# The last two heads' gradient stores cut into 120 and 8 partitions, in a decode transformer layer's forward and backward pass

## The chip, the cores and the metric

The kernel runs on one core of a Trainium2 chip. The metric is the time of one execution on the device in microseconds (us), as the median of the runs of a kernel. The engines are named as in the profile: PE (TensorE matmul), PEld (its weight load), DVE (VectorE), ACT (ScalarE), POOL (GpSimd) and SP (SyncE). SP, ACT and POOL also issue DMA transfers, each into a queue of its own, and 16 DMA engines carry out what the queues hold.

## The reference

One decoding step of a transformer layer for a batch of 4, with everything in bf16, forward and backward. Cut to what matters:

```
B=4, H=32 heads, Sk=4096 cached positions, Dh=128, D=512, F=1792
h   = x + softmax(q . k_cache / sqrt(Dh)) . v_cache @ wo,    q = layernorm(x) @ wq
out = h + (silu(n @ w1) * (n @ w3)) @ w2,                    n = layernorm(h)
returns out, and the gradients of x, k_cache, v_cache, wq, wo, w1, w3, w2 for grad_out
```

By bytes the caches are nearly all of it. k_cache and v_cache hold 4 x 32 heads of 4096 x 128 numbers, 1 MB per head and cache, so 128 MB each; k_cache is read once and v_cache twice, and the two gradients of the same size are written. The gradient of v_cache for a head is the outer product of the head's probabilities with the gradient of its attention output; that of k_cache is the outer product of the gradient of its scores with its query.

## The kernel before

A head's 4096 x 128 block is one SBUF tile of 128 partitions: partition p holds the positions 32p to 32p+31, which are 8 KB in a row in memory. Such a tile lies in a "slot" of SBUF; there are 22 slots, and a program-side list `free` says which ones can be given out again. The order of the instructions on each engine is the order in which the program writes them down.

The kernel has three stages. The first goes over all heads for the forward attention. The middle one computes the output projection and the feed-forward block, forward and backward. The third, which the change touches, goes once more over all 128 heads `s`, with batch index `b = s % 4` and head index `h = s // 4`; so the last two are b = 2 and 3 of h = 31. For every head:

- `prefetch` and `load_V2` (L749) load V for heads to come, from SP's queue.
- `front(s + 1)` transposes V of the next head on PE (L739), copies it back to SBUF on ACT (`V_T`, L740), and multiplies it on PE with the output gradient (L1070).
- `store_late(nc.scalar)` issues, from ACT's queue, the two stores of the head before: the gradient of v (`gv`, to `out_3`) and of k (`gk`, to `out_2`), 1 MB each (L1106). It then gives both slots free.
- `back(s)` forms `gv` and `gk` of this head on DVE (two outer products at L1077, and small steps at L1090 and L1093 between them) and appends them to `late`.
- Heads 0 and 1 are stored at once, from POOL's queue, in place of that.
- `step` puts in pieces of the weight gradients (`side_work`), whose stores of some 0.9 to 1 MB go from POOL's queue, besides two stores of 4 rows from SP's queue (L964 and L987).

After the last `back`, one more `store_late(nc.scalar)` issues the stores of head 127, and there is no work left for `step`.

A DMA instruction tells of its landing by a semaphore. Eight semaphores go round for the transfers of SP's and ACT's queues; before an issue the program waits until the transfer that had the same semaphore before, eight issues earlier, has landed. The last loads of V come well ahead of the end, so that at the end all eight go round among ACT's stores.

Of the kernel before, what the change touches and what calls it, by code (L numbers as in the profile page):

```python
# [24 lines left out]
def kernel(  # L25
# [23 lines left out]
    P = nc.NUM_PARTITIONS  # L49

    B = A_x.shape[0]
    D = A_x.shape[-1]
    H = A_k_cache.shape[1]
# [33 lines left out]
    def rows_of(ap):  # L87
        return ap.rearrange("(p j) d -> p j d", p=P)
# [83 lines left out]
    def ones_window(col):  # L172
# [11 lines left out]
                          in_=rowg[:, None, :, None].to_broadcast([P, 4, 8, 4]))  # L184
# [691 lines left out]
    with ExitStack() as c2:  # L876
# [226 lines left out]
        def store_late(eng):  # L1103
            b, h, gv, gk = late.popleft()
            for out_ap, sl in ((out_3, gv), (out_2, gk)):
                eng.dma_start(out=rows_of(out_ap[b, h]), in_=sl.heads())  # L1106
                sl.give()

        def prefetch(s):
# [6 lines left out]
        for s in range(NH):  # L1116
            prefetch(s + 1)
            if s + 1 < NH:
                if s + 1 not in V2s and s + 1 not in VTs:
                    load_V2()  # L1120
                front(s + 1)
            if late:
                store_late(nc.scalar)
            back(s)
            if s < 2:
                store_late(nc.gpsimd)
            if s >= S0:
                step("s", 1 if s < S0 + 44 else 2 + (s % 3 == 0))
        store_late(nc.scalar)
        step("s", 400)  # L1130

# [29 lines left out]
```

## Time and profile before

| | |
|---|---|
| runs (3) | 1748.7, 1748.4, 1747.94 us; median 1748.4 |
| profiled execution | 1748.7 us; span from its first to its last instruction 1746.9 us |
| busy share of the span | PE 76%, PEld 64%, DVE 72%, ACT 55%, POOL 16% |
| DMA | 707.85 MB, mean 405 GB/s |
| share of the 16 DMA engines' span by queue | q1 (SP's) 59.5%, q10 (ACT's) 36.4%, q0 (POOL's) 2.5%, instruction pages 0.6% |
| mean TensorE clock granted | 0.75 |

How to read it. The shares are means over three stages with different limits; what the change is worth is read from the end of the third stage. The page cuts the span into 40 slices of 43.7 us and gives for each the busy tenths of the engines and of the DMA engines, and the bytes moved. The view of the DMA queues does the same for any stretch, cut into 40 slices, and names the transfers issued in it with their time from issue to landing. The timeline gives each instruction's start and duration; "ACTq" is ACT's sequencer, which waits and issues while the engine itself computes nothing.

### The profile page before, as it was taken

To read this page: it belongs to the slowest core of one execution; us is meant where nothing else is said; L and a number is where in the kernel's file an instruction comes from. 1 tells how busy PE (TensorE), PEld (TensorE's weight loads), DVE (VectorE), ACT (ScalarE), POOL (GpSimd) and SP (SyncE) were. 2 spreads that over 40 slices of the span, in tenths; PEclk is the share of its full clock that TensorE was granted. 3 is DMA by queue.
4 is the path that set the end of the run, shared out by engine and by line. 5 is a ranking of instruction groups with operands and counts; after the bars stand their busy time and mean duration, and the time that the engine had idled before them with its cause. 6 is when DMAs were issued, how large, how long until landed. Compare 5 with 4: busy or idle time off the path is not lost.

```text
span 1746.9 us, 43817 instructions
## 1 busy us (share of the span) xinstructions
PE 1324.8 (76%) x18993; PEld 1113.0 (64%) x18993; DVE 1253.1 (72%) x1382; ACT 956.8 (55%) x1463; POOL 278.9 (16%) x552
## 2 busy tenths in 40 slices
PE   5889888888888889877777876666868767766773
PEld 4667666677666667767776875554656555655563
DVE  5989899889998996555667577557466655656484
ACT  3455445445444544655555555556756666666663
POOL 2333333333333330100000000000000010011000
PEclk8999999999999999755555556676556655556555
DMA  9999999999999999789999999999999999999998
GB/s 398 410 418 418 419 418 419 419 412 418 417 416 397 418 407 360 287 356 411 418 413 404 422 418 412 388 397 395 425 424 419 401 414 413 411 423 417 417 415 343
DMA packets 107122, 707.85 MB, mean 405 GB/s; under 512 B 11232, under 2 KB 18920, under 8 KB 23984
## 3 DMA queue, kind: packets, MB, share of 16 engines
q1 hardware_dynamic: 67280, 422.68, 59.5%
q10 hardware_dynamic: 36288, 264.26, 36.4%
q0 software_dynamic: 3360, 18.11, 2.5%
q8 instruction: 149, 2.44, 0.5%
q14 instruction: 45, 0.37, 0.1%
HBM read 422.58 MB, written 282.34 MB: 404 GB/s over the span
## 4 chain that ended last, share of the span: by engine, by line
DMA 36%; ACT 10%; PE 9%; DVE 4%; issue 2%; ACTq 1%; SPq 0%; POOL 0%; DVEq 0%; POOLq 0%
DMA out_dram<-gk 15%; DMA out_dram<-gv 9%; ACT VT L740 7%; DMA V<-in_A_v_cache_dram 6%; PE pt_tps L739 4%; DMA wq<-in_A_wq_dram 2%; DVE gv L1077 2%; PE dq_ps L902 1%; DMA out_dram<-gwo 1%; PE rep_ps L1054 1%; DVE gk L1077 1%; ACTq L1106 1%; DMA w<-in_B_w_dram 1%; DMA w2a<-in_B_w_dram 1%; DMA out_dram<-gwq 1%
## 5 line engine op out<-in xcount | busy, mean ns | idle before, releaser
L740 ACT COPY VT<-pt_tps 128x1024 bf16<-128x1024 bf16 x512 | 491.9, 1016 | 212.9 <-PE pt_tps L739 132.9
L739 PE MATMUL pt_tps<-ident_b,V 128*128 128x128 bf16 x4096 | 451.1, 292 | 88.5 <-ACT VT L740 88.5
L739 PEld LDWEIGHTS <-V 128*128 128x128 bf16 x4096 | 401.0, 138 | 176.2 <-issue 160.5
L1077 DVE TENSOR_TENSOR gv<-P,reps 128x4096 bf16<-128x4096 bf16 x128 | 292.9, 2288 | 200.7 <-DMA out_dram<-gk 95.8
L1077 DVE TENSOR_TENSOR gk<-dS,reps 128x4096 bf16<-128x4096 bf16 x128 | 293.4, 2292 | 67.8 <-DMA out_dram<-gv 39.8
L421 DVE TENSOR_TENSOR PK<-Kn,PK 128x4096 bf16<-128x4096 bf16 x128 | 302.9, 2366 | 35.9 <-POOL PK L417 35.9
L436 PE MATMUL M_ps<-PK,Vn 128*128 128x130 bf16 x4096 | 285.4, 222 | 45.1 <-DMA Vn<-in_A_v_cache_dram 44.2
L436 PEld LDWEIGHTS <-Vn 128*128 128x128 bf16 x4096 | 252.4, 99 | 65.4 <-DMA Vn<-in_A_v_cache_dram 59.1
L328 DVE STREAM_TRANSPOSE KT<-Kn 128x512 f32<-128x512 f32 (+1 forms) x321 | 250.9, 798 | 0.5 <-issue 0.5
L323 ACT COPY KT<-pt_tps 128x1024 bf16<-128x1024 bf16 x128 | 129.4, 1012 | 186.9 <-PE pt_tps L322 155.3
L1070 PE MATMUL dP_ps<-dOT_bf,VT 128*128 128x1 bf16 x4096 | 152.4, 166 | 67.4 <-ACT VT L740 65.7
L1070 PEld LDWEIGHTS <-VT 128*128 128x128 bf16 x4096 | 141.0, 104 | 79.8 <-ACT VT L740 77.8
L336 POOL COPY zq<-qT_bf 128x2 bf16<-128x2 bf16 x128 | 152.3, 1190 | 0.0
L1073 POOL COPY P<-P_all 128x64 bf16<-128x64 bf16 x128 | 43.2, 352 | 592.9 <-DVE gv L1077 592.9
L417 POOL COPY PK<-P_all 128x64 bf16<-128x64 bf16 x128 | 32.4, 253 | 437.0 <-ACT P_all L411 431.7
L1090 DVE TENSOR_SCALAR dSt<-dP_ps,c_rep 128x32 f32<-128x32 f32 x128 | 31.6, 246 | 97.0 <-PE dP_ps L1070 96.8
L411 ACT COPY P_all<-pt_P 32x64 bf16<-32x64 bf16 x256 | 52.1, 203 | 58.0 <-PE pt_P L407 55.7
L322 PE MATMUL pt_tps<-ident_b,Kn 128*128 128x128 bf16 x1024 | 80.7, 223 | 0.7 <-DVE qrep L282 0.7
L446 PE MATMUL kP_ps<-PK,onesw 128*32 128x512 bf16 x1024 | 79.2, 386 | 0.0
L322 PEld LDWEIGHTS <-Kn 128*128 128x128 bf16 x1024 | 62.2, 100 | 26.5 <-issue 26.5
L1057 ACT CAST reps<-rep_ps 128x512 bf16<-128x512 f32 x64 | 37.5, 586 | 70.9 <-PE rep_ps L1054 59.7
L400 ACT ACTIVATE Pn<-E,rl 128x1024 bf16<-128x1024 f32 x64 | 73.7, 1152 | 2.8 <-DVE rl L397 2.8
(234 smaller groups left out, 1231.5 us busy)
## 6 DMA issues: line engine op xcount, KB each, us to landing
Kn<-in_A_k_cache_dram SPq DMA_DIRECT2D x128, 1024.0 KB, 14.9
Vn<-in_A_v_cache_dram SPq DMA_DIRECT2D x128, 1024.0 KB, 15.2
V<-in_A_v_cache_dram SPq DMA_DIRECT2D x128, 1024.0 KB, 10.6
out_dram<-gv ACTq DMA_DIRECT2D x126, 1024.0 KB, 12.8
out_dram<-gk ACTq DMA_DIRECT2D x126, 1024.0 KB, 15.3
wq<-in_A_wq_dram SPq DMA_DIRECT2D x8, 1024.0 KB, 11.1
out_dram<-gw POOLq DMA_DIRECT2D x6, 896.0 KB, 11.9
wo<-in_A_wo_dram SPq DMA_DIRECT2D x4, 1024.0 KB, 12.1
```

Of the source, the lines that this page charges most:

```text
L322: nc.tensor.transpose(pt[:, i, :], Kn[:, c * GW + i, :], ident_b[:])
L323: nc.scalar.copy(out=KT[:, c * GW:(c + 1) * GW, :], in_=pt[:])
L328: nc.vector.transpose(out=KT[:, c * w_:(c + n) * w_], in_=Kn[:, c * w_:(c + n) * w_])
L336: nc.gpsimd.tensor_copy(out=zq[gi % 2][hl][:, 32:132:67], in_=qT_bf[:, s:s + 1].to_broadcast([P, 2]))
L400: nc.scalar.activation(out=st["Pn"][:], in_=st["E"][:, :, None, :].to_broadcast([P, JQ, 4, 32]), func=AF.Copy, scale=rl[:])
L421: nc.vector.tensor_tensor(out=PK[:, :, 0:Dh].rearrange("p j (r t) -> p j r t", t=2), in0=Ks[s].heads().rearrange("p j (r t) -> p j r t", t=2),
L436: nc.tensor.matmul(hold["M"][:], lhsT=Vn[:, j, :], rhs=PK[:, j, :], start=(j == 0), stop=(j == SJ - 1))
L446: nc.tensor.matmul(hold["kP"][32 * q:32 * (q + 1), :, :], lhsT=ones_window(w), rhs=PK[:, j0:j0 + 4, 0:Dh], start=(w == 0 and c == 0), stop ...
L739: nc.tensor.transpose(pt[:, i, :], Vn[:, g * GW + i, :], ident_b[:])
L740: nc.scalar.copy(out=VT[:, g * GW:(g + 1) * GW, :], in_=pt[:])
L1070: nc.tensor.matmul(dP_ps[:, j:j + 1], lhsT=VT[:, j, :], rhs=dOT_bf[:, s:s + 1], start=True, stop=True)
L1077: nc.vector.tensor_tensor(out=dst.rearrange("p j (r t) -> p j r t", t=2), in0=col2[:, :, None, :].to_broadcast([P, SJ, Dh // 2, 2]), in1=r ...
```

## The change

The stores of the last two heads are each issued in two parts: partitions 0 to 119 and partitions 120 to 127. All other stores stay as they were. Where four DMA instructions were issued from ACT's queue at the end (gv and gk of heads 126 and 127), there are eight, each part of 120 rows followed by its part of 8 rows; the bytes, their places and the slots are the same. The lines behind the changed ones move down by 4, so that the store's line is L1106 before and L1110 after.

```diff
         def store_late(eng):
             b, h, gv, gk = late.popleft()
             for out_ap, sl in ((out_3, gv), (out_2, gk)):
-                eng.dma_start(out=rows_of(out_ap[b, h]), in_=sl.heads())
+                cut = [0, 120, P] if h == H - 1 and b >= B - 2 else [0, P]
+                for p0, p1 in zip(cut[:-1], cut[1:]):
+                    eng.dma_start(out=rows_of(out_ap[b, h])[p0:p1], in_=sl.heads()[p0:p1])
                 sl.give()
```

## The prediction

> **What bounds the kernel now.** I read the page's slices first, then its queue table, and then the last 47 us, because the change touches nothing earlier. In the page's second part one digit is a fortieth of the span (43.7 us).
>
> ```profile
> DMA  9999999999999999789999999999999999999998
> GB/s 398 410 418 418 419 418 419 419 412 418 417 416 397 418 407 360 287 356 411 418 413 404 422 418 412 388 397 395 425 424 419 401 414 413 411 423 417 417 415 343
> ...
> q10 hardware_dynamic: 36288, 264.26, 36.4%
> ```
>
> The DMA engines are at 9 tenths or more nearly throughout, so the kernel is bound by bytes, and nothing on PE, DVE, ACT or POOL counts at its end. Only the last slice is low: 343 GB/s against 415 to 417 before it. q10 is ACT's queue. It carries 252 stores of 128 rows: 252 x (128 packets of 8 KB + 16 closing packets) = 36288. So each of 16 engines gets 8 packets and one closing packet of every store.
>
> The timeline of ACT, 1711 to 1728 us, shows the last issues (start, time, what), the last six being gv and gk of heads 125, 126 and 127.
>
> ```profile
> 1721.13 0.34 ACTq L1106 DMA_DIRECT2D out_dram<-gv  x1
> 1721.16 1.04 ACT L740 COPY VT<-pt_tps 128x1024 bf16<-128x1024 bf16 x1
> 1721.56 0.93 ACTq L1106 DMA_DIRECT2D out_dram<-gk  x1
> 1722.59 1.33 ACTq L1106 DMA_DIRECT2D out_dram<-gv  x1
> 1724.01 1.17 ACTq L1106 DMA_DIRECT2D out_dram<-gk  x1
> 1725.27 1.19 ACTq L1106 DMA_DIRECT2D out_dram<-gv  x1
> 1726.56 1.21 ACTq L1106 DMA_DIRECT2D out_dram<-gk  x1
> ```
>
> DVE's last product starts at 1723.47 and takes 2.29 us. All that follows is storing. The DMA view of 1735 to 1747 us (slices of 0.3 us) shows how the storing ends, and that of 1740.95 to 1745.3 its last piece:
>
> ```profile
> GB/s 437 382 410 437 382 437 437 437 219 218 164 164 137 137 137 137 82 55 55 27 27 27 27 27 27 27 27 27 27 27 0 27 27 27 0 0 0 0 0 0
> DMA packets 226, 1.57 MB, mean 131 GB/s; under 512 B 34, under 2 KB 34, under 8 KB 34
> ```
>
> ```profile
> DMA packets 15, 0.11 MB, mean 24 GB/s; under 512 B 2, under 2 KB 2, under 8 KB 2
> ```
>
> One engine moves 27 GB/s (437/16). So eight engines are done by 1737.4, six are left at 1738.0, three at 1739.8, two at 1740.1, and from 1740.9 to 1745.2 one works alone. Its last 15 packets are 13 of 8 KB and two closing ones in 4.3 us, 0.31 us per 8 KB packet, which is the pace of the others: it isn't slow there, it is late, by about 13 packets against the second latest and 25 against the first eight. The last store was issued at 1726.56, and the DMA view of 1726 to 1728 gives its landing:
>
> ```profile
> out_dram<-gk ACTq DMA_DIRECT2D x1, 1024.0 KB, 19.1
> ```
>
> It lands at 1745.65, and the span ends 1.25 us later, at 1746.9. (Profiled execution: 1748.7; span plus 1.8. The runs' median is 1748.4, 0.3 lower. I subtract from the median.)
>
> **The change, part by part.** Four stores of 128 rows (gv and gk of heads 126 and 127) become four of 120 rows and four of 8. The program order says that nothing else moves: PE, DVE, POOL and SP have the same instructions, ACT has four issues more, at its very end.
>
> *Four issues more on ACT.* 4 x 0.34 to 1.33 us (rows above) = 1.4 to 5.3 us. ACT has nothing after its VT copy at 1721.16, and no engine waits for ACT any more. They cost nothing as long as packets are queued: the last store sits 19.1 us between issue and landing, where the first store of the phase, on idle engines (issued at 747.6), took 3.9 us.
>
> *The waits in front of them.* Eight completion semaphores go round, and an issue waits until the store eight issues earlier has landed. With eight issues where four were, this wait moves later: the 120 rows of head 127's gv wait for head 124's gv (issued 1716.58, 12.0 us to land: 1728.6), its 8 rows for head 124's gk (1717.02 + 14.0 = 1731.0), the 120 rows of gk for head 125's gv (between its neighbours, one store of 2.45 us apart: 1733.4), and its 8 rows for head 125's gk (1721.56 + 14.3 = 1735.9). Behind each on ACT stand only the remaining parts. An early engine asks for gk of head 127 about 8 x 0.306 = 2.45 us before its end at 1737.4, so at 1735.0. Issued at 1733.4, the packets are there about 0.9 us later (3.9 less 8 packets and a landing of 0.5) or, if the issue takes its 1.2 us, at 1735.5. Early engines may idle 0.5 us; they have 3.5 us to spare before 1740.9. The last 8 rows, issued at 1735.9, land by 1735.9 + 3.9 = 1739.8 even if they took as long as a whole store. So: 0 us, hidden by the late engines.
>
> *What the cut does to the engines.* This is the whole effect. A store of 128 rows runs on 16 engines. The page's packet count also tells of small ones: q1's 67280 packets come out only if the two stores of 4 rows (L964, L987) have 4 closing packets each, not 16. So the row count sets the number of engines, and the nearest rule through 128 on 16 and 4 on 4 is the largest number up to 16 that divides the rows: 120 on 15, 8 on 8. One engine then has no packet of the last four stores: 4 x (8 x 0.306 + 0.006) = 9.8 us less for it. Eight engines get one packet and a closing one more per store: 4 x 0.31 = 1.25 us more.
>
> If the engine left out is the late one, it ends at 1745.2 - 9.8 = 1735.4. The end is then set by the second latest: 1740.9 if it isn't among the eight, 1740.9 + 1.25 = 1742.2 if it is; between the two the third and fourth, from 1740.1 to 1740.4, plus 1.25, give up to 1741.6. Gain 3.05 to 4.3 us, middle 3.6. Following packets (each starts where the last one of its engine ended), I find that the engines of the 4-row store at L987 aren't those that also fetch instruction pages, and that the late one takes no such pages either and is none of those four, while the latest of the others does fetch them; if the eight include the four engines of that small store, the second latest is more likely not hit. I take 3.6: 1748.4 - 3.6 = 1744.8.
>
> The Trainium skill, DMA: Bandwidth & Descriptors, section "Rules for kernel authors", speaks against the change: two transfers to disjoint sets of partitions gain nothing, since both go over all 16 engines. By that rule the late engine keeps its load, and the sum is zero or a loss. The same page, section "Why a DMA increments its semaphore by 16 and not by 1", states the divisor rule (100 partitions on 10 engines) and that the lowest-numbered engines are taken; by it the engine left out is the last, number 15. Its section "Latency and other measured facts" says that engines 7 and 15 are usually the slower ones; the trace gives no numbers of engines, so it shows one late engine without saying which. With 15 the sum is the gain above; with 7 it is a loss of 1.25 us.
>
> What a measurement can tell from no change here is about 0.2%, 3.5 us; the runs of before lie within 0.8 us.
>
> **The rivals.**
>
> *A, forecast (0.70): the late engine is the one relieved.* For it: it keeps its lag through a stretch in which every engine works at the same pace, so its lag comes from its own history, and it is none of the small store's engines. Against: 14 others could be left out. 1744.1 to 1745.4, by itself with the runs' spread 1743.9 to 1745.6.
>
> *B (0.21): another engine is relieved.* The late one then keeps its 8 packets per store, and takes 4 x 0.31 us more if it is among the eight. 1748.4 to 1749.65. For it: the count of engines says nothing of which; a cut between rows 119 and 120 spares one engine only.
>
> *C, slower (0.09): 120 rows go to fewer than 15 engines.* If the number must be a power of two, 8 engines take 15 rows each. Their extra is 4 x (7 x 0.306 + 0.31) = 9.8 us: on the second latest 1740.9 + 9.8 = 1750.7, a span 5.5 us longer, 1753.9; on the late one itself 1758.2. It decides from 10 engines on: 12 rows each give 4 x (4 x 0.306 + 0.31) = 6.1 us, so the second latest ends at 1747.0, past 1745.2. Both known row counts, 128 and 4, are powers of two with powers of two for engines, so the page doesn't exclude it.
>
> **How the numbers follow.** The likeliest is A with 1744.8. In A the gain passes 3.5 us where the second latest isn't among the eight; I give that 0.49 of the 0.70. Faster 0.49, within 0.2% 0.21 + 0.21 = 0.42, slower 0.09. The range has to reach into B, since A alone is 0.70: from 1743.9 to 1749.6.
>
> **What would show it.** q10's packets count the engines: 36288 - 4 x 144 + 4 x (120 + 15) + 4 x (8 + 8) = 36316 for 15 and 8; 36352 if all parts go to 16; 36288 again for 8 and 8. In the DMA view of the end, the stretch of 27 GB/s alone should shrink from 4.3 us to about 1, and the last packet lie 3 to 4.3 us nearer to DVE's last product. I am wrong in the mechanism if that stretch stays at 4 us or more (B), and in the sum if ACT's last issue comes later than 1738 or the slices before 1737 fall below 400 GB/s: then the moved waits starve the engines.

## Result and profile after

The changed kernel is slower: 1754.62 us, the median of four runs (1753.77 to 1756.67), against 1748.55 us (1747.94 to 1749.19) before. The ratio is 1.0036, with a 95% interval of 1.0019 to 1.0054, so the loss is 6.1 us where a gain of 3.6 was forecast. The profiled execution took 1754.06 us, its span 1752.3.

These are the page's slices and ACT's queue of the changed kernel, to be laid beside the same lines of before.

```profile
DMA  9999999999999999689999999999999999999997
GB/s 398 409 419 418 419 418 419 419 415 418 413 417 394 418 407 356 275 358 416 417 419 413 422 418 409 392 382 417 425 423 411 401 411 405 420 419 416 418 415 298
...
q10 hardware_dynamic: 36316, 264.26, 36.5%
```

The queue has 36316 packets, the number that the prediction worked out for parts of 120 rows on 15 engines and parts of 8 rows on 8. So the engines were counted rightly. The last slice is at 298 GB/s in place of 343, and the slice before it is unchanged at 415: the loss is at the very end. (Slices 16 and 17, in the middle stage, differ too; the change issues nothing there.)

The timeline of ACT shows the last issues of the changed kernel (start, duration, instruction; x2 is a part of 120 rows and its part of 8).

```profile
1725.18 2.48 ACTq L1110 DMA_DIRECT2D out_dram<-gv  x2
1727.76 3.60 ACTq L1110 DMA_DIRECT2D out_dram<-gk  x2
1731.45 5.46 ACTq L1110 DMA_DIRECT2D out_dram<-gv  x2
1737.01 3.56 ACTq L1110 DMA_DIRECT2D out_dram<-gk  x2
```

Before, the last issue began at 1726.56. Now the last two lie between 1737.01 and 1740.57. The waits have moved as the prediction said, but they are longer than it worked out (it had the last at 1735.9). On DVE the last product starts later as well, in this execution. The first line is the kernel before, the second the changed one:

```profile
1723.47 2.29 DVE L1077 TENSOR_TENSOR gk<-dS,reps 128x4096 bf16<-128x4096 bf16 x1
1725.53 2.29 DVE L1077 TENSOR_TENSOR gk<-dS,reps 128x4096 bf16<-128x4096 bf16 x1
```

Of these 2.06 us, 1.6 are there already at the product before (1722.36 in place of 1720.73), and the rest is a wait for PE; the first part of the change is issued at 1725.18. In the profiles of the experiments the same product starts anywhere from 1722.48 to 1728.45. So profiles are compared below by their drain: the span's end less the start of this product. It is 23.43 us before and 26.77 us after, 3.3 us more.

The DMA views of the drain show where that comes from. The first fence is the kernel before from 1727 to 1737 us, the second the changed one from 1730 to 1742 us, in both while ACT's last stores are moving on nearly all engines.

```profile
DMA packets 584, 4.26 MB, mean 426 GB/s; under 512 B 64, under 2 KB 64, under 8 KB 64
## 3 DMA queue, kind: packets, MB, share of 16 engines
q10 hardware_dynamic: 584, 4.26, 101.5%
```

```profile
DMA packets 496, 3.51 MB, mean 293 GB/s; under 512 B 67, under 2 KB 67, under 8 KB 67
## 3 DMA queue, kind: packets, MB, share of 16 engines
q10 hardware_dynamic: 496, 3.51, 89.5%
```

Read the rate and the share at the end of the last line together. The engines are busy for 89.5% of this time, so they don't mainly wait for packets; yet they move 293 GB/s, not 426. What remains is that a packet takes longer. The share gives it: before, 1.015 x 16 engines x 10 us over 584 - 64 = 520 packets of 8 KB is 0.31 us each; after, 0.895 x 16 x 12 us over 429 is 0.40 us. That is a mean over the whole stretch, in which some stores of 128 rows are still on their way. It hides two kinds of packets: in the trace's list of packets, 292 of the 429 took less than 0.34 us, as all 520 did before, and the other 137 took longer, most often about 0.6 us.

The end of the drain, the changed kernel from 1741 to 1752 us in slices of 0.275 us:

```profile
GB/s 328 179 298 268 209 417 298 387 238 209 238 0 89 30 60 30 30 60 60 60 60 60 60 30 60 60 0 30 30 30 30 30 30 30 30 0 0 0 0 0
```

30 is one packet in a slice. Most engines are done at about 1744.5 and not at 1737.4; two engines go on to about 1748.1, and one alone to 1750.6.

### The profile page after: what moved, and what is told of

It is laid out like the page before. It is cut to its first block, busy times and chain, and to the rows that moved or that the text cites. A ratio compares the mean times of both kernels' runs of the same rounds, so it can differ in the third digit from the quotient of the medians.

```text
span 1752.3 us, 43821 instructions
## 1 busy us (share of the span) xinstructions
PE 1321.2 (75%) x18993; PEld 1116.8 (64%) x18993; DVE 1252.8 (71%) x1382; ACT 956.6 (55%) x1463; POOL 283.2 (16%) x552
## 3 DMA queue, kind: packets, MB, share of 16 engines
q10 hardware_dynamic: 36316, 264.26, 36.5%
q8 instruction: 149, 2.44, 0.5%
## 4 chain that ended last, share of the span: by engine, by line
DMA 36%; PE 10%; ACT 9%; DVE 5%; issue 2%; ACTq 1%; POOL 0%; DVEq 0%; SPq 0%
DMA out_dram<-gk 15%; DMA out_dram<-gv 11%; DMA V<-in_A_v_cache_dram 7%; ACT VT L740 7%; PE pt_tps L739 4%; DVE gv L1077 3%; DMA wq<-in_A_wq_dram 1%; DVE gk L1077 1%; DMA out_dram<-gwo 1%; PE dq_ps L902 1%; PE rep_ps L1054 1%; DMA w2a<-in_B_w_dram 1%; PE dP_ps L1070 1%; ACTq L1110 1%; PE M_ps L436 1%
## 5 line engine op out<-in xcount | busy, mean ns | idle before, releaser
L1073 POOL COPY P<-P_all 128x64 bf16<-128x64 bf16 x128 | 47.6, 386 | 592.7 <-DVE gv L1077 592.7
L354 PE MATMUL S_ps<-KT,W 128*32 128x256 bf16 x1536 | 74.6, 285 | 0.1
```

What stands on the lines that cost most here:

```text
L354: nc.tensor.matmul(st["S"][32 * c:32 * (c + 1), :], lhsT=lhsT, rhs=rhs, start=(hl == 0 and k == 0), stop=(hl == G - 1 and k == 3), tile_po ...
```

## Experiments

Each edit is one to the changed kernel, and concerns only the stores of the last two heads unless said. Three theories stood at first: the parts take longer because of how their rows lie over the engines ("spread"; with the later runs "ports", "dealing"); the moved waits starve the engines ("waits"); or nothing is slow, and the late engine is one of the eight that take a ninth packet ("late alone"). Each ratio is against the kernel before, run again beside the experiment: its median was 1748.81 us for the first four experiments, 1748.76 for the next four and 1748.3 for the last two.

**Parts of columns: eight issues and their waits, with 128 rows in each.**

```diff
-                cut = [0, 120, P] if h == H - 1 and b >= B - 2 else [0, P]
-                for p0, p1 in zip(cut[:-1], cut[1:]):
-                    eng.dma_start(out=rows_of(out_ap[b, h])[p0:p1], in_=sl.heads()[p0:p1])
+                cut = [0, 30, SJ] if h == H - 1 and b >= B - 2 else [0, SJ]
+                for j0, j1 in zip(cut[:-1], cut[1:]):
+                    eng.dma_start(out=rows_of(out_ap[b, h])[:, j0:j1], in_=sl.heads()[:, j0:j1])
```

> The stores of the last two heads are cut by columns instead of by partitions: 128 rows of 7.5 KB and 128 rows of 0.5 KB. There are again eight issues at the end, with the same semaphores and the same bytes in each part, but every part has 128 rows, so nothing changes in which engine takes which rows. Theory Spread (a store of 120 rows is slow because its rows fall on the engines otherwise than those of 128 rows do): 1748.5 to 1749.5 us, packets at their usual pace up to the end. Theory Waits (the waits that move later starve the engines): as the changed kernel, 1753.5 to 1755.5 us, with gaps between packets. Theory Late alone (the late engine is one of the eight that take the 8 rows, and nothing else): 1748.5 to 1749.5 us.

Measured: 1748.07 us, ratio 0.9997 (0.9988 to 1.0006), drain 21.16 us. It has the same eight issues, the same bytes in each part and the same waits behind eight semaphores, and no loss can be measured. Its last issues in the timeline, and its DMA view from 1728 to 1738 us:

```profile
1730.06 2.54 ACTq L1110 DMA_DIRECT2D out_dram<-gv  x2
1732.90 2.75 ACTq L1110 DMA_DIRECT2D out_dram<-gk  x2
```

```profile
DMA packets 951, 4.13 MB, mean 413 GB/s; under 512 B 107, under 2 KB 443, under 8 KB 836
```

413 GB/s. Its last pair begins at 1732.90 and not at 1737.01, since the stores that it waits for land sooner. So the late issues of the changed kernel are a consequence of slow packets and not their cause. The theory of the waits falls.

**The parts of 120 rows alone: rows 120 to 127 aren't stored.**

```diff
-                cut = [0, 120, P] if h == H - 1 and b >= B - 2 else [0, P]
+                cut = [0, 120] if h == H - 1 and b >= B - 2 else [0, P]
```

> The last two heads' stores have rows 0 to 119 only; rows 120 to 127 of those four blocks are left out. Four issues at the end, as before the change, so no wait moves, and no engine takes a ninth packet. Theory Spread: still slower than before, 1751 to 1753.5 us (1754.6 less 1.25 us for the ninth packets, and up to 2 us if the eight waits cost something too), with 8 KB packets of 0.6 us among those of 0.31. Theory Waits: 1748.5 us. Theory Late alone: 1748.5 us, because the late engine then has its 8 packets per store as before.

Measured: 1753.94 us, 1.0029 (1.0017 to 1.0041), drain 29.32 us. This kernel has as many issues as the kernel before, no wait moved, and 0.26 MB less to store; it loses nearly the whole, 0.4 us more than the range expected for "spread". So the waits and the ninth packets aren't needed for a loss. Its DMA view from 1727 to 1737 us:

```profile
DMA packets 447, 3.26 MB, mean 326 GB/s; under 512 B 49, under 2 KB 49, under 8 KB 49
```

**Cut at row 112: the parts of 112 and of 16 rows both run on 16 engines.**

```diff
-                cut = [0, 120, P] if h == H - 1 and b >= B - 2 else [0, P]
+                cut = [0, 112, P] if h == H - 1 and b >= B - 2 else [0, P]
```

> The cut lies at 112: 112 rows are 7 on each of 16 engines, 16 rows one on each, so every engine has 8 packets per head's block as before, but in eight issues, and with consecutive rows on an engine if that is how rows are dealt out whenever there aren't 128. Theory Spread by consecutive rows: slower than before, 1751 to 1755 us. If the 15 engines in place of 16 are what costs: 1748.5 to 1749.5 us. Theory Waits: 1753.5 to 1755.5 us. Theory Late alone: 1748.5 us, since no engine gets more than before.

Measured: 1754.66 us, 1.0034 (1.0023 to 1.0046), drain 26.82 us, and 36352 packets on the queue: 16 engines for both parts, and seven packets plus one, so eight for every engine, as before the change. Its DMA view from 1728 to 1740 us:

```profile
DMA packets 470, 3.11 MB, mean 259 GB/s; under 512 B 91, under 2 KB 91, under 8 KB 91
```

The loss is about that of the change. So a loss of this size needs neither an engine that is left out nor eight with one packet more: all engines have equal loads here, and are slow.

**Cut at row 64.**

```diff
-                cut = [0, 120, P] if h == H - 1 and b >= B - 2 else [0, P]
+                cut = [0, 64, P] if h == H - 1 and b >= B - 2 else [0, P]
```

> The cut lies at 64: each half is 4 rows on each of 16 engines, and each engine has 8 packets per block. The Trainium skill (SBUF: State Buffer, Door 1: the DMA port swizzle) states that partitions 0 to 63 lie behind 8 of the 16 ports and 64 to 127 behind the other 8, so that half the bandwidth is reached. Theory Spread through ports: a half's 4 rows take about 0.6 us per packet, so up to twice the 2.45 us per block while both halves keep in step: 1752 to 1758 us, more than with 120 and 8. Theory Spread by the engines' number alone: 1748.5 to 1749.5 us. Theory Waits: 1753.5 to 1755.5 us. Theory Late alone: 1748.5 us.

Measured: 1751.55 us, 1.0014 (1.0004 to 1.0024), drain 24.85 us. Slow again (270 GB/s from 1727 to 1739 us), but it costs less than the change, where more was expected: a miss in size. The two halves of a head were in flight together, and by the next two runs the lower half is slow by itself. That each half is slow for what it shares with itself and not with the other, and that this is why it costs less, is argued, not shown.

**The same size of store on two sets of partitions.** The first stores only rows 0 to 63 of the last two heads, the second only rows 32 to 95; the other rows aren't stored. Rows, bytes, issues and packets are the same (36032 on the queue in both).

```diff
-                cut = [0, 120, P] if h == H - 1 and b >= B - 2 else [0, P]
+                cut = [0, 64] if h == H - 1 and b >= B - 2 else [0, P]
```

> The last two heads' stores have partitions 0 to 63 only; 64 to 127 of those four blocks are left out. Four issues, 64 rows, 16 engines with 4 packets each. To be read beside the kernel with partitions 32 to 95. The Trainium skill (SBUF: State Buffer, Door 1: the DMA port swizzle) states that these rows lie behind 8 ports. Theory Ports: two engines meet at each port, 8 KB packets of 0.45 to 0.6 us in place of 0.31 while the four stores run, 200 to 300 GB/s. Theory Dealing (any row count other than 128 is dealt out in a way that costs, whichever rows): the same here as with partitions 32 to 95. Time with half of the last 4 MB left out: at the usual pace 1743.5 to 1744.5 us (the late engine has 16 packets fewer, 4.9 us); with slow packets 1744.5 to 1747.5.

```diff
-                cut = [0, 120, P] if h == H - 1 and b >= B - 2 else [0, P]
+                cut = [32, 96] if h == H - 1 and b >= B - 2 else [0, P]
```

> The last two heads' stores have partitions 32 to 95 only; the others of those four blocks are left out. Four issues, 64 rows, 16 engines with 4 packets each, as many bytes as with partitions 0 to 63. If rows are dealt out in order, four to an engine, engines 0 to 7 have partitions 32 to 63 and engines 8 to 15 partitions 64 to 95, which by the Trainium skill's table of ports (SBUF: State Buffer, Door 1: the DMA port swizzle) are 16 different ports, one for each engine. Theory Ports: packets at 0.31 us as with 128 rows, above 400 GB/s, and 1743.5 to 1744.5 us. Theory Dealing: packets as slow as with partitions 0 to 63, and the same time as that kernel.

Measured: 1746.93 us, 0.9986 (0.9976 to 0.9997), drain 22.98 us, for rows 0 to 63; 1745.46 us, 0.9977 (0.9966 to 0.9989), drain 15.25 us, for rows 32 to 95. The second is 1 us above the range expected for packets at the usual pace. The times lie close together; the DMA views of the stretches in which these stores run do not. Rows 0 to 63, from 1729 to 1738 us:

```profile
DMA packets 311, 2.03 MB, mean 226 GB/s; under 512 B 63, under 2 KB 63, under 8 KB 63
## 3 DMA queue, kind: packets, MB, share of 16 engines
q10 hardware_dynamic: 311, 2.03, 91.6%
```

Rows 32 to 95, from 1732 to 1737 us:

```profile
DMA packets 317, 2.11 MB, mean 421 GB/s; under 512 B 60, under 2 KB 60, under 8 KB 60
## 3 DMA queue, kind: packets, MB, share of 16 engines
q10 hardware_dynamic: 317, 2.11, 101.4%
```

The same 2 MB go at 226 GB/s from one set of partitions and at 421 from another. A packet takes 0.916 x 16 x 9 us / 248 = 0.53 us in the first, 1.014 x 16 x 5 us / 257 = 0.32 us in the second. In the first, the trace's list has 98 of the 248 packets under 0.34 us and 118 of 0.58 to 0.70, about twice as long; in the second, all 257 are under 0.34. Nothing differs but which partitions are read, and with them which rows of the output are written. So the place of the rows sets the pace; that it is the place in SBUF and not that in memory is argued, since no run moved one without the other. The Trainium skill, SBUF — State Buffer, section "Door 1: The DMA port swizzle (why [64,N] ≈ [32,N])", says that transfers reach SBUF by 16 ports of 8 partitions each, and that 0 to 63 lie behind eight of them and 64 to 127 behind the other eight; partitions 32 to 95 lie behind all 16. The two rates, one about half the other, agree with it.

For 120 rows all 16 ports are within reach, and still the packets are slow. The Trainium skill, DMA: Bandwidth & Descriptors, section "The descriptor swizzle", says that a transfer of 128 rows is dealt out so that each engine works at a port of its own; the 426 GB/s of before agree. For other row counts that section gives no assignment. If 120 rows are dealt out in order, eight consecutive partitions to an engine, an engine works at two ports in turn, and shares them with others; two meet from time to time. That fits 293 to 326 GB/s, between the two rates above, but the trace doesn't tell which engine moved which row: for 120 rows this is argued.

**Parts of 49 rows: seven engines only (rows 49 to 127 aren't stored).**

```diff
-                cut = [0, 120, P] if h == H - 1 and b >= B - 2 else [0, P]
+                cut = [0, 49] if h == H - 1 and b >= B - 2 else [0, P]
```

> The last two heads' stores have partitions 0 to 48 only; the others are left out. By the divisor rule (the Trainium skill, DMA: Bandwidth & Descriptors, Why a DMA increments its semaphore by 16 and not by 1) 49 rows go on 7 engines with 7 packets each, and those are the first seven. It tells which engine is late. If it is the eighth, it has none of the last four stores, ends 9.8 us earlier and no longer sets the end: no stretch of one engine alone, last landing about 20 to 22 us after the start of DVE's last product becomes 15 to 18. If it is among the first seven, it has 28 packets in place of 32, and the stretch alone stays at 3 us or more.

Measured: 1751.28 us, 1.0020 (1.0007 to 1.0033), drain 23.04 us, 36288 - 4 x 144 + 4 x (49 + 7) = 35936 packets, so seven engines. The DMA view from 1722 to 1754 us, in slices of 0.8 us:

```profile
GB/s 379 451 399 440 379 451 399 307 225 215 174 174 143 133 123 133 123 133 133 174 133 92 92 82 92 51 41 51 51 10 0 0 0 0 0 0 0 0 0 0
```

The nine engines without a share stop when they have done head 125's stores, and the seven go on until about 1745.6. The last part of head 125's gk lands at 1737.38, and the four stores of 49 rows at 1739.53, 1741.68, 1743.86 and 1745.99 us, each about 7 x 0.31 = 2.15 us after the one before: the engine that ended head 125's gk takes its seven packets of every store without a pause, at full pace. So the late engine is one of these seven. One of the two signs that the expectation gave for this came: the last landing is still 21.7 us after the start of DVE's last product. The other didn't: the last 51 GB/s are two engines and not one, since a second one lands at 1745.54. If the engines taken are the lowest in number, as the Trainium skill says in DMA: Bandwidth & Descriptors, section "Why a DMA increments its semaphore by 16 and not by 1", then it is neither number 15 nor the eighth. Which of the seven it is stays open.

**Only the last head cut.**

```diff
-                cut = [0, 120, P] if h == H - 1 and b >= B - 2 else [0, P]
+                cut = [0, 120, P] if h == H - 1 and b >= B - 1 else [0, P]
```

> Only the last head is stored in parts of 120 and 8; head 126 in one part as before. Theory Ports or Dealing: two stores at the slower pace in place of four, about half of the whole change's price, 1750 to 1752.5 us beside 1748.6. If the price comes once, from the last landing alone: the same as the whole change, 1753.5 to 1755.5 us. Late engine alone: 0.6 us more than before.

Measured: 1751.31 us, 1.0018 (1.0009 to 1.0027), drain 24.31 us: half the dose, half the loss (+2.6 us against the +6.1 of the change). Its DMA views show both paces in one execution: from 1727 to 1735 us, stores of 128 rows, then from 1736 to 1743 us, the cut ones.

```profile
DMA packets 460, 3.36 MB, mean 420 GB/s; under 512 B 50, under 2 KB 50, under 8 KB 50
...
DMA packets 277, 1.96 MB, mean 280 GB/s; under 512 B 38, under 2 KB 38, under 8 KB 38
```

**The change and its parts of 120 rows, side by side.** To see what the parts of 8 rows cost, the changed kernel as it is was measured again beside the kernel that leaves rows 120 to 127 out; the edits are those shown above.

> The changed kernel once more, beside a kernel that has the 120-row parts only. Theory Ports (two engines at one port slow the 120-row parts): slower than before by 5 to 6 us, 1753.5 to 1755 us, nearly all of it there without the 8-row parts too. If the ninth packets on the late engine carry a share: 1.25 us more than the 120-row parts alone.

> The 120-row parts alone; rows 120 to 127 of the last two heads' blocks are left out. Theory Ports: slower than before by 4 to 5.5 us. The difference to the changed kernel of this call is what the 8-row parts and their waits cost: 1.25 us if the late engine takes a ninth packet of each block, 0 if it doesn't.

Measured: the change 1753.65 us, 1.0035 (1.0020 to 1.0049), drain 28.12 us; the 120 rows alone 1757.91 us, 1.0046 (1.0029 to 1.0064), drain 30.78 us. The change came out the same as in its first measurement. The 120 rows alone lose 9.6 us where 4 to 5.5 were expected, a miss in size, and 5.1 in their first measurement. So the loss is there without the parts of 8 rows, and their 1.25 us can't be seen in these times: the intervals overlap, and the kernel without them is the slower one, if either. What they cost on the late engine is read from the trace in the next section.

## Why the prediction was wrong

*What bounds the kernel.* Right: the end of the third stage is set by the stores' drain, and within it by a late engine.

*"Four issues more on ACT" and "The waits in front of them", 0 us each.* Right, by the parts of columns: eight issues and eight waits, ratio 0.9997. But the sign by which the prediction meant to find them wrong was a bad one. It said that the waits starve the engines if ACT's last issue comes after 1738 or the slices before 1737 fall below 400 GB/s. Both came true, and the waits are not the cause: a slow landing makes a late issue as surely as a late issue makes a slow landing. The busy share tells them apart, since engines at 89.5% don't starve.

*"What the cut does to the engines".* This step failed, twice.

The main failure is a term that isn't in the sum: what other engines' parts do to a packet's duration. The step counted packets and gave each its 0.306 us. The number of packets was right (36316); the price was not. The prediction read 0.31 us from a trace whose large stores all have 128 rows, and took over as a fixed price what held for that pattern. The row that could have warned was missing: the trace of before shows no large store with another row count. This should have been bounded from both sides, as it was done for the waits.

Where the time goes can be followed on the engine that ends last. In the trace, each engine that takes part in a store reports its share done by one count on the store's semaphore: 16 counts for 128 rows, 15 for 120 and 8 for 8. Before, the last count of each store comes 2.44 us (eight packets) after that of the store before it, down to the end. In the changed kernel the last counts of head 125's gv and gk come at 1733.95 and 1740.04, 6.09 us apart. Both are the same engine, since the other 15 are through with gk by 1732.88, and followed by their starts and ends its eight packets take 0.62 to 0.94 us each. This store has 128 rows and isn't cut; the other engines are in the parts of 120 and 8 rows meanwhile. Then the late engine does its own 36 packets of cut stores in 11.20 us, 0.31 us each. So it pays 3.65 us for being held up on an uncut store, and 4 x 0.31 = 1.25 us for four ninth packets: 4.9 us, where the sum had a gain.

The same reading of the other traces:

| kernel | time lost on stores of 128 rows, us | its packets of the last stores: number, us |
|---|---|---|
| before | 0.0 | 32, 9.7 |
| parts of columns | 0.1 | 64 (half of them 0.5 KB), 9.9 |
| the change | 3.7 | 36, 11.2 |
| the change again | 4.1 | 36, 11.6 |
| 120 rows alone | 6.7 | 32, 9.8 |
| 120 rows alone again | 7.2 | 32, 9.8 |
| only the last head cut | 2.4 | 18, 5.7 |
| cut at row 64 | 2.6 | 32, 10.1 |
| rows 0 to 63 | 4.3 | 16, 4.9 |
| rows 32 to 95 | 0.1 | 16, 4.9 |
| rows 0 to 48 | 1.4 | 28, 8.6 |

The second column is what the steps from one last count to the next exceed 2.44 us by, from head 124's gv to the last uncut store; the third is what follows. (With the cut at row 112 two engines end close together, at 1737.11 and 1737.73 for head 125's gk, and the steps can't be told apart; the late one needs over 5 us for that store too.) The late engine is held up in every kernel whose last stores have slow packets, and not in those whose last stores keep the usual pace.

The second failure is the engine. The forecast's case needed the late engine to be the one without packets. In the changed kernel's record of landings, the part of 120 rows of the last gv lands at 1748.16 us and its 8 rows at 1748.49, one packet later; the last gk's 8 rows land last of all, at 1751.24. The engine that ends last is thus one that takes the 8 rows, one of the eight, as in rival B. The stretch alone, 2.5 us, matches neither the 4 us named for B nor the 1 us named for the forecast, because the second latest engine is held up too: it reports 2.6 us before the last one (1748.60), where it was 4.4 us before.

*The rivals.* B had the engine and its 1.25 us for the ninth packets right, but lacks the 3.65 us. C had the sign right by another mechanism: it let the number of engines fall, and 15 and 8 was the number all along. None of the three had a pace that changes. The rule that the prediction weighed against itself, which the skill's page states for two halves of the partitions, that two transfers gain nothing over one, stood on the right side of zero: the cut gained nothing and cost 6.1 us. Its reason, that all 16 engines are used either way, is not what happened: the parts ran on 15 and 8.

*What stays open.* The medians differ by 6.1 us, the late engine's account gives 4.9, and the two drains differ by 3.3. Between the last two stands that, before it is held up, the late engine of the changed kernel's profile is 1.6 us nearer to DVE's last product: head 125's gv lands 8.42 us after the product's start, 9.98 before. The drain of the kernel before is known from one profile, and those of the kernels with 120 rows on both heads range from 26.77 to 30.78; the time lost on uncut stores ranges there from 3.7 to 7.2 us, and why it is longer without the parts of 8 rows is open. So is why the late engine, slow while it reads an uncut store beside the others' cut parts, is at full pace once it reads cut parts itself, and how it came to be late.

No version here that stores everything beats the kernel before; only the parts of columns measure the same.

## What to carry to other kernels

A packet's duration isn't a fixed price: here it depended on which rows all the engines read at the time, and the engine that set the end paid on a store that wasn't cut. Before a transfer is cut by partitions, ask which partitions each engine will read and behind which ports they lie; a cut along the columns keeps all 128 rows in each part, and cost nothing measurable here. And when a drain gets longer, read the engines' busy share with the rate: busy and slow is a matter of the packets, as here; idle and slow would be one of the issues, which no run here shows.

## What the runs showed of the hardware

- Half the partitions can have the whole rate: 32 to 95 moved 421 GB/s, 0 to 63 moved 226.
- Stores with a row count other than 128 over nearly all partitions were slower too: 326 GB/s for 120 rows alone, 293 for 120 and 8, 259 for 112 and 16, against 426 for 128.
- An engine's packets of an uncut store of 128 rows took 0.62 to 0.94 us each, in place of 0.31, while the others worked on parts of 120 and 8 rows; the same engine's packets of these parts then took 0.31.
- The engine that ends last is not the one without a share in a part of 120 rows, and is one of the seven that share a store of 49 rows.
- The start of the last product varied by 6 us from one profile to another (1722.48 to 1728.45), as much as the whole effect under study.
